# Sketched attention and a ReGLU feed-forward on one core: one interleaved program in place of two stages

## The chip, the core and the metric

The kernel runs on one core of a Trainium2 chip. A core has five engines that run side by side, each in its own order: PE (TensorE, matrix products into PSUM), DVE (VectorE), ACT (ScalarE), POOL (GpSimd) and SP (which here only issues transfers). The metric is the device time of one execution, in microseconds (us).

## What is computed

Queries, keys and values have 4 batches, 4 heads, 1088 tokens and 32 numbers a head. A sketch turns each head's 32 numbers into two vectors a and b of 8 numbers; their outer product is a feature vector of 64. Attention is linear in it, and its output is the input of a gated feed-forward layer (128 -> 1536 -> 128):

```python
def phi(x):
    a = np.einsum('rd,bhsd->bhsr', S1, x)
    b = np.einsum('rd,bhsd->bhsr', S2, x)
    return np.einsum('bhsi,bhsj->bhsij', a, b).reshape(*x.shape[:-1], r * r)
q_p, k_p = (phi(q), phi(k))
kv = np.einsum('bhsf,bhsd->bhfd', k_p, v)
z = np.sum(k_p, axis=2)
num = np.einsum('bhsf,bhfd->bhsd', q_p, kv)
den = np.einsum('bhsf,bhf->bhs', q_p, z)[..., None] + 1e-06
x = (num / den)            # then heads side by side: 4352 tokens x 128
out = (np.maximum(x @ w_gate, 0.0) * (x @ w_val)) @ w_out
```

## The kernel before

The program has two stages, and a scheduler orders the instructions of each engine.

**Attention** (L91 to L237) goes batch by batch. A batch's 1088 tokens are nine chunks, eight of 128 tokens and one of 64, with token s on partition s of its chunk; so the loads (L107 to L116) move runs of 32 numbers, 128 bytes each. For each key chunk PE transposes it as an fp32 matrix (L135), DVE copies the result out of PSUM (L137), PE applies the sketch (L140, an fp32 product, which stands as two matrix instructions in the trace), ACT copies that out (L142), POOL forms the outer products `kp` (L154), and PE adds up z (L144, `zbig`) and kv (L158) over the chunks. Between keys and queries ACT copies the sums out (L165 to L176) and PE folds z into the sketch matrix `s_bd_ext` (L172), so that the query product also yields what the denominator needs. Each query chunk then goes through transpose (L183), sketch (L188), outer product on POOL (L195), transpose of the features on PE (L202), copy on DVE (L208), product with kv (L211), the denominator (POOL L215, DVE L222, POOL L223, DVE L225), the division (DVE L228), another PE transpose (L236) and the copy into `xT` (ACT L237). `xT` is x with its 128 features on the partitions, for all 4352 tokens.

**Feed-forward** (L239 to L278) takes `xT` in chunks of 512 tokens (eight, and one of 256). For each of the 12 slices j of the 1536 hidden numbers: a gate product of 512 columns (L250), its ReLU on ACT (L252), a value product (L255), and on DVE the product of both into `ht` (L256). Twelve products with 512 columns each (L260) then give the output with its features on partitions; ACT copies it (L263), PE transposes it back in four pieces (L272), ACT scales it (L273), SP stores it (L275).

## Time and profile before

| | |
|---|---|
| runs | 224.64 and 225.14 us, median 224.89 |
| span of the profiled execution, first to last instruction | 223.3 us; so some 1.3 to 1.8 us of a run lie outside the span |
| busy in the span | PE 179.1, DVE 106.2, ACT 103.2, POOL 82.1 us |
| mean granted PE clock over the span | 0.973 |
| first PE instruction | at 14.2 us |
| first FFN product of the unbroken stretch | at 144.2 us |
| transfers | 61776 packets, 57152 of them under 512 bytes, 9.18 MB |

A busy share is the time in which an engine had an instruction in flight; matrix instructions overlap each other, so a busy PE may still have room. Rows of groups give, after the shapes and the count, busy us and the mean ns of one instruction, then the idle time ahead of them and who ended it. Rows of the timeline give start, length, engine and line.

### The profile page before, as it was taken

To read this page: it belongs to the slowest core of one execution; us is meant where nothing else is said; L and a number is where in the kernel's file an instruction comes from. 1 tells how busy PE (TensorE), PEld (TensorE's weight loads), DVE (VectorE), ACT (ScalarE), POOL (GpSimd) and SP (SyncE) were. 2 spreads that over 40 slices of the span, in tenths; PEclk is the share of its full clock that TensorE was granted. 3 is DMA by queue.
4 is the path that set the end of the run, shared out by engine and by line. 5 is a ranking of instruction groups with operands and counts; after the bars stand their busy time and mean duration, and the time that the engine had idled before them with its cause. 6 is when DMAs were issued, how large, how long until landed. Compare 5 with 4: busy or idle time off the path is not lost.

```text
span 223.3 us, 3087 instructions
## 1 busy us (share of the span) xinstructions
PE 179.1 (80%) x906; PEld 105.7 (47%) x906; DVE 106.2 (48%) x290; ACT 103.2 (46%) x307; POOL 82.1 (37%) x187
## 2 busy tenths in 40 slices
PE   0018999659949989689997795599999999999992
PEld 0005666437727667366674552234444444444460
DVE  0002003333114431224422154369998989989981
ACT  0021243112433213332234362158898988988981
POOL 8402578997378853158632385000000000000000
PEclk9999999999999999999999999559999999999998
DMA  7999989765494100000000000000110110110110
GB/s 95 156 125 135 156 107 84 72 23 44 72 52 72 28 0 0 3 0 1 0 1 3 0 0 1 0 0 3 47 48 0 47 51 0 47 42 6 50 47 23
DMA packets 61776, 9.18 MB, mean 41 GB/s; under 512 B 57152, under 2 KB 61504, under 8 KB 61760
## 3 DMA queue, kind: packets, MB, share of 16 engines
q1 hardware_dynamic: 39952, 6.69, 17.8%
q0 software_dynamic: 19568, 2.30, 17.0%
q10 hardware_dynamic: 2240, 0.01, 0.7%
q8 instruction: 7, 0.11, 0.2%
q14 instruction: 9, 0.07, 0.1%
HBM read 9.06 MB, written 2.23 MB: 51 GB/s over the span
## 4 chain that ended last, share of the span: by engine, by line
PE 60%; POOL 18%; DMA 7%; issue 5%; DVE 4%; ACT 4%; SPq 0%; ACTq 0%; POOLq 0%
PE v_ps L255 12%; PE ot_ps L260 10%; PE g_ps L250 10%; POOL qp L195 8%; PE ab_ps L140 7%; DMA k<-in_k_dram 4%; PE zbig_ps L144 4%; POOL den L223 3%; POOL bw L215 3%; PE tr_ps L183 3%; PE kv_ps L158 2%; DMA s_bd<-in_S_dram 2%; PE xtsz_ps L236 2%; PE ndq_ps L211 2%; PE ab_ps L188 2%
## 5 line engine op out<-in xcount | busy, mean ns | idle before, releaser
L256 DVE TENSOR_TENSOR ht<-g_sb,v_ps 128x512 f16<-128x512 f16 (+1 forms) x108 | 67.3, 656 | 8.1 <-PE v_ps L255 4.0
L252 ACT ACTIVATE g_sb<-g_ps 128x512 f16<-128x512 f32 (+1 forms) x108 | 59.1, 583 | 11.5 <-PE g_ps L250 7.9
L255 PE MATMUL v_ps<-xT,wv_sb 128*128 128x512 f16 (+1 forms) x108 | 40.7, 379 | 0.8 <-DVE ht L256 0.4
L250 PE MATMUL g_ps<-xT,wg_sb 128*128 128x512 f16 (+1 forms) x108 | 40.9, 382 | 0.0
L260 PE MATMUL ot_ps<-ht,wo_sb 128*128 128x512 f16 (+1 forms) x108 | 39.8, 374 | 0.2 <-DVE ht L256 0.2
L154 POOL TENSOR_TENSOR kp<-ab_sb 128x256 f16<-128x256 f32 (+1 forms) x36 | 22.2, 623 | 23.8 <-ACT ab_sb L142 20.6
L135 PE MATMUL tr_ps<-ident,k 128*128 128x128 f32 (+1 forms) x36 | 14.7, 435 | 17.8 <-DMA k<-in_k_dram 14.2
L188 PE MATMUL ab_ps<-s_bd_ext,tr_sb 128*128 128x96 f32 (+1 forms) x72 | 25.3, 455 | 4.5 <-ACT s_bd_ext L175 2.6
L195 POOL TENSOR_TENSOR qp<-ab_sb 128x256 f16<-128x256 f32 (+1 forms) x36 | 22.5, 625 | 13.1 <-ACT ab_sb L190 12.3
L142 ACT COPY ab_sb<-ab_ps 128x64 f32<-128x64 f32 (+1 forms) x36 | 7.6, 211 | 41.0 <-PE ab_ps L140 31.8
L140 PE MATMUL ab_ps<-s_bd,tr_sb 128*128 128x64 f32 (+1 forms) x72 | 23.5, 431 | 2.3 <-DMA s_bd<-in_S_dram 2.3
L188 PEld LDWEIGHTS ab_ps<-s_bd_ext,tr_sb 128*128 128x128 f32 (+1 forms) x72 | 17.1, 298 | 9.6 <-ACT ab_sb L190 5.4
L137 DVE COPY tr_sb<-tr_ps 128x128 f32<-128x128 f32 (+1 forms) x36 | 9.6, 275 | 25.4 <-PE tr_ps L135 21.9
L222 DVE TENSOR_REDUCE den<-bw 128x4 f32<-128x32 f32 (+1 forms) x36 | 6.6, 184 | 30.6 <-POOL bw L215 30.3
L190 ACT COPY ab_sb<-ab_ps 128x96 f32<-128x96 f32 (+1 forms) x36 | 8.6, 238 | 25.7 <-PE ab_ps L188 22.4
L140 PEld LDWEIGHTS ab_ps<-s_bd,tr_sb 128*128 128x128 f32 (+1 forms) x72 | 17.5, 305 | 4.7 <-issue 3.1
L208 DVE COPY qpt<-ndq_ps 128x256 f16<-128x256 f16 (+1 forms) x36 | 10.0, 277 | 17.8 <-PE ndq_ps L202 17.2
L135 PEld LDWEIGHTS tr_ps<-ident,k 128*128 128x128 f32 (+1 forms) x36 | 8.0, 229 | 20.9 <-issue 14.4
L250 PEld LDWEIGHTS <-wg_sb 128*128 128x128 f16 x108 | 11.1, 103 | 13.2 <-issue 4.7
L260 PEld LDWEIGHTS <-wo_sb 128*128 128x128 f16 x108 | 10.6, 98 | 14.1 <-issue 3.8
L255 PEld LDWEIGHTS <-wv_sb 128*128 128x128 f16 x108 | 10.7, 99 | 12.6 <-issue 2.9
L237 ACT COPY xT<-xtsz_ps 128x128 f16<-128x128 f16 (+1 forms) x36 | 9.4, 261 | 14.8 <-PE xtsz_ps L236 14.7
(44 smaller groups left out, 207.5 us busy)
## 6 DMA issues: line engine op xcount, KB each, us to landing
k<-in_k_dram SPq DMA_DIRECT2D x16, 128.0 KB, 3.5
q<-in_q_dram SPq DMA_DIRECT2D x16, 128.0 KB, 4.6
out_dram<-o_sb SPq DMA_DIRECT2D x8, 256.0 KB, 2.3
v<-in_v_dram POOLq DMA_DIRECT2D x16, 64.0 KB, 3.4
wg_sb<-in_moe_w_gate_dram POOLq DMA_DIRECT2D x1, 384.0 KB, 5.9
wv_sb<-in_moe_w_val_dram POOLq DMA_DIRECT2D x1, 384.0 KB, 7.5
wo_sb<-in_moe_w_out_dram POOLq DMA_DIRECT2D x1, 384.0 KB, 11.0
s_bd<-in_S_dram ACTq DMA_DIRECT2D x8, 1.0 KB, 5.6
```

The source lines that it names most:

```text
L135: nc.tensor.transpose(tr_ps[:, :c], k4[:c, ci].rearrange("s h d -> s (h d)"), ident[:c, :c])
L137: nc.vector.tensor_copy(out=tr_sb[:, :c], in_=tr_ps[:, :c])
L140: nc.tensor.matmul(ab_ps[:c, 0:2 * HR], tr_sb[:, :c], s_bd, start=True, stop=True)
L154: nc.gpsimd.tensor_tensor(out=kp[:c], in0=a_bc, in1=b_bc, op=ALU.mult)
L188: nc.tensor.matmul(ab_ps[:c], tr_sb[:, :c], s_bd_ext, start=True, stop=True)
L195: nc.gpsimd.tensor_tensor(out=qp[:c], in0=a_bc, in1=b_bc, op=ALU.mult)
L208: nc.vector.tensor_copy(out=qpt[:, :, :c], in_=qpt_ps[:, :, :c])
L250: nc.tensor.matmul(g_ps[:, :cs], wg_sb[:, j], xT[:, c0:c0 + cs], start=True, stop=True)
L252: nc.scalar.activation(out=g_sb[:, :cs], in_=g_ps[:, :cs], func=ACTF.Relu)
L255: nc.tensor.matmul(v_ps[:, :cs], wv_sb[:, j], xT[:, c0:c0 + cs], start=True, stop=True)
L256: nc.vector.tensor_tensor(out=ht[:, j, :cs], in0=g_sb[:, :cs], in1=v_ps[:, :cs], op=ALU.mult)
L260: nc.tensor.matmul(ot_ps[:, :cs], wo_sb[:, j], ht[:, j, :cs], start=(j == 0), stop=(j == NJ - 1))
```

## The change

The program is rewritten under a manual schedule: each engine runs its instructions in the order in which the source issues them.

- **Layout.** Of a batch, tokens 0 to 1023 are laid out eight to a partition (C = 8), so a load moves runs of 256 numbers, 1 KB each (`load_main`). The last 64 tokens of the four batches form one "rest" group of 256 tokens (`load_rest`). S1 is loaded 16 times (`s1r`).
- **Transposes.** fp32 matrix transposes on PE are replaced by 32x32 block transposes on DVE, before the sketch product (`t1`) and after it (`t2`), 512 columns at a time. The sketch product (`ab`) has the sketch as its weights and the transposed tokens as 512 fp32 columns.
- **Denominator.** It divides the vector a ahead of the outer product (`den`), so the product with kv yields x directly, with its features on the partitions, and `x` copies it into `xT`.
- **Feed-forward.** A token group is 512 tokens (two per batch), and a step `F` is two slices j: two gate and two value products of 512 columns, two ReLUs, one DVE product of 1024 columns. The output products take `ht` as weights and `wo` as 128 columns: eight for each step, which give the output with its tokens on partitions (`out`, two steps behind `gv`). The transposes back are gone. There are 48 such steps and three for the rest group.
- **Order.** The attention of the next group is cut into tasks, which `at` places at slots among these steps; whole slots come ahead of a step's `gv`, half slots between its `gv` and the `out` of two steps ago. All tasks take turns in one PSUM bank (`ps_m`).

Three places show what stands where now. First, the start on POOL. Before, the weights' transfers come ahead of all else; the names with numbers are buffers.

```order
L83 DMA wg_sb<-in_moe_w_gate_dram 128x1536
L85 DMA wv_sb<-in_moe_w_val_dram 128x1536
L87 DMA wo_sb<-in_moe_w_out_dram 128x12x128
L109 DMA v_150<-in_v_dram 128x8x32 x4
L113 DMA v_150<-in_v_dram 64x4x32
L129 COPY s_bd_ext<-s_bd 128x64 [waits DMAHW4_49,DMAHW5_49,DMAHW3_49,DMAHW6_49,DMAHW2_49,DMAHW7_49,DMAHW1_49,DVE_49]
```

Now a copy that waits for the loads of `s1r` stands ahead of them, and the first outer products (`kpr` of the rest group, `kp` of batch 0) behind them.

```order
L85 DMA v_sb_108<-in_v_dram 128x4x256
L120 COPY s1rep<-s1r 128x128 [waits DMAHW4_49,DMAHW6_49,DMAHW3_49,DMAHW7_49,DMAHW2_49,DMAHW0_49]
L121 DMA wg<-in_moe_w_gate_dram 128x1536
L122 DMA wv<-in_moe_w_val_dram 128x1536
L123 DMA wo<-in_moe_w_out_dram 128x12x128
L85 DMA v_sb_109<-in_v_dram 128x4x256
L85 DMA v_sb_110<-in_v_dram 128x4x256
L85 DMA v_sb_111<-in_v_dram 128x4x256
L176 TENSOR_TENSOR kpr<-abr 128x512 [waits DVE_49]
L176 TENSOR_TENSOR kp<-abk 128x512 [waits DVE_49]
```

So POOL's arithmetic moved behind six of its own transfers and one wait for ACT's.

Second, DVE in the feed-forward. Before, nothing stands among its products:

```order
L256 TENSOR_TENSOR ht<-g_sb,v_ps 128x512 [waits PE_49] x4
L256 TENSOR_TENSOR ht<-g_sb,v_ps 128x512 [waits PE_49,Activation_49] x92
L256 TENSOR_TENSOR ht<-g_sb,v_ps 128x256 [waits PE_49,Activation_49] x12
```

Now, for one query group (batch 1, first half; `abq` is `t2`, `dn` and `rd` belong to `den`, `pt` is `tre`):

```order
L263 TENSOR_TENSOR kv_bd_210<-m_ps,maskkv 128x128
L296 STREAM_TRANSPOSE qt<-q_sb_105 128x512 [waits DMAHW5_49]
L398 TENSOR_TENSOR ht<-g_sb,v_ps 128x1024 [waits DVE_49,PE_49,Activation_49]
L274 TENSOR_TENSOR wst_180<-m_ps,maskw 128x16x8 [waits PE_49,Pool_49]
L310 STREAM_TRANSPOSE abq<-m_ps 128x512
L320 TENSOR_REDUCE dn<-bw_184 128x16 [waits Pool_49]
L322 RECIPROCAL rd<-dn 128x16 [waits DVE_49]
L398 TENSOR_TENSOR ht<-g_sb,v_ps 128x1024 [waits PE_49,Activation_49] x2
L349 COPY pt<-m_ps 128x1024 [waits PE_49]
```

The attention's DVE work moved from ahead of the feed-forward to between its products, and each waits its turn behind a `ht`.

Third, PE. Before, only the output's own transposes stand among the feed-forward's products (`ot_2105` is one chunk's output):

```order
L250 LDWEIGHTS wg_sb
L250 MATMUL g_ps<-xT,wg_sb 128x512 [waits Activation_49]
L260 LDWEIGHTS wo_sb
L260 MATMUL ot_ps<-ht,wo_sb 128x512
L272 LDWEIGHTS ot_2105 [waits Activation_49]
L272 MATMUL ott_ps<-ident_96,ot_2105 128x128 [waits PE_49]
```

Now, at the same query group as above, the transposes of its features (`tr`, L339), which wait for POOL, stand behind a step's value products and ahead of the output products of two steps ago:

```order
L390 LDWEIGHTS wg
L390 MATMUL g_ps<-xT,wg 128x512 [waits Activation_49]
L395 LDWEIGHTS wv
L395 MATMUL v_ps<-xT,wv 128x512 [waits DVE_49]
L339 LDWEIGHTS qp [waits Pool_49]
L339 MATMUL m_ps<-ident,qp 128x128 [waits DVE_49]
L409 LDWEIGHTS ht
L409 MATMUL o_ps<-wo,ht 128x128
```

PE takes its instructions in this order, so all feed-forward products behind that L339 wait with it.

The core of the diff (the removed lines are the body of the kernel above; masks, identities and fills are left out):

```diff
+    ctx.enter_context(tc.manual_schedule())
...
+    ps_g = ctx.enter_context(tc.tile_pool(name="ps_g", bufs=2, space=bass.MemoryType.PSUM))
+    ps_v = ctx.enter_context(tc.tile_pool(name="ps_v", bufs=2, space=bass.MemoryType.PSUM))
+    ps_o = ctx.enter_context(tc.tile_pool(name="ps_o", bufs=1, space=bass.MemoryType.PSUM))
+    ps_m = ctx.enter_context(tc.tile_pool(name="ps_m", bufs=1, space=bass.MemoryType.PSUM))
...
+    def load_main(eng, dst, src, b):
+        eng.dma_start(out=dst, in_=src[b, :, 0:SM, :].rearrange("h (p c) d -> p h (c d)", c=C))
...
+    nc.scalar.dma_start(out=s16[0:R], in_=S1[:, None, :].to_broadcast([R, 4, D]))
+    nc.scalar.dma_start(out=s16[R:2 * R], in_=S2[:, None, :].to_broadcast([R, 4, D]))
+    load_rest(nc.sync, kr, k)
+    load_main(nc.sync, k_sb[0], k, 0)
+    load_main(nc.gpsimd, v_sb[0], v, 0)
+    load_rest(nc.scalar, vr32, v)
+    for x in range(128 // R):
+        nc.scalar.dma_start(out=s1r[x * R:(x + 1) * R], in_=S1)
+    load_main(nc.sync, q_sb[0], q, 0)
+    for b in range(1, B):
+        load_main(nc.sync, k_sb[b], k, b)
+        load_main(nc.sync, q_sb[b], q, b)
+    load_rest(nc.sync, qr, q)
...
+    nc.gpsimd.tensor_copy(out=s1rep, in_=s1r[:, None, :].to_broadcast([128, 4, D]))
+    nc.gpsimd.dma_start(out=wg, in_=moe_w_gate.rearrange("m (j f) -> m j f", j=NJ))
+    nc.gpsimd.dma_start(out=wv, in_=moe_w_val.rearrange("m (j f) -> m j f", j=NJ))
+    nc.gpsimd.dma_start(out=wo, in_=moe_w_out.rearrange("(j f) m -> f j m", f=128))
+    for b in range(1, B):
+        load_main(nc.gpsimd, v_sb[b], v, b)
...
+    def rest_k():
+        kt = a_t.tile([128, E * H * 32], FP32, name="ktr")
+        nc.vector.transpose(kt, kr.rearrange("p h (e d) -> p e h d", e=E))
+        ps = ps_g.tile([128, 512], FP32, name="g_ps")
+        nc.tensor.matmul(ps[:, 0:E * H * 32], sk[:, 0].rearrange("p a b f -> p (a b f)"), kt,
+                         start=True, stop=True)
+        nc.vector.transpose(abr.rearrange("p x f -> p (x f)"), ps[:, 0:E * H * 32])
+        outer(nc.gpsimd, kpr, abr, 0, R, E * H)
+    class K:
...
+        def t1(self, hf):
+            if hf == 0:
+                self.kt = a_t.tile([128, 2, GT], FP32, name="kt")
+            nc.vector.transpose(
+                self.kt[:, hf],
+                k_sb[self.b][:, :, hf * GC * D:(hf + 1) * GC * D].rearrange(
+                    "p h (c d) -> p c h d", d=D),
+            )
+        def ab(self, pool=ps_m, name="m_ps"):
+            self.ps = pool.tile([128, 512], FP32, name=name)
+            for hf in range(2):
+                nc.tensor.matmul(self.ps, sk[:, hf].rearrange("p a b f -> p (a b f)"),
+                                 self.kt[:, hf], start=(hf == 0), stop=(hf == 1))
+        def t2(self):
+            self.absb = a_ab.tile([128, GC * H, 32], FP32, name="abk")
+            nc.vector.transpose(self.absb.rearrange("p x f -> p (x f)"), self.ps)
+            self.kp = a_kp.tile([128, 2, GC * H, R * R], FP16, name="kp")
+        def phi(self, hf, eng, lo=0, hi=GC):
+            sl = slice(lo * H, hi * H)
+            outer(eng, self.kp[:, hf, sl], self.absb[:, sl], hf * 16, hf * 16 + R, (hi - lo) * H)
...
+        def kvz(self):
+            b = self.b
...
+                    nc.tensor.matmul(
+                        m[:, p * 64:p * 64 + 64],
+                        kpr[rows, e * H + 2 * p:e * H + 2 * p + 2].rearrange("s h f -> s (h f)"),
+                        vr[rows, 2 * p:2 * p + 2, e * D:(e + 1) * D],
+                        start=first, stop=False, skip_group_check=True)
...
+                        ab = self.absb[:, c * H:(c + 1) * H]
+                        nc.tensor.matmul(
+                            m[:, 128:192].rearrange("f (a h j) -> f a h j", a=2, h=H),
+                            ab.rearrange("s h f -> s (h f)"),
+                            ab.rearrange("s h (a f) -> s a h f", a=2)[:, :, :, R:2 * R],
+                            start=False, stop=c == GC - 1, skip_group_check=True)
...
+        def evac(self):
+            self.zd = a_sm.tile([128, 2 * H * R], FP32, name="zd")
+            nc.vector.tensor_tensor(
+                out=self.zd, in0=self.m[:, 128:192],
+                in1=maskz.rearrange("p a h j -> p (a h j)"), op=ALU.mult)
...
+        def w(self):
+            b = self.b
+            for hf in range(2):
+                nc.tensor.matmul(self.m[:, 192:224], s1rep.rearrange("p a d -> p (a d)"),
+                                 self.zd[:, hf * H * R:(hf + 1) * H * R],
+                                 start=hf == 0, stop=hf == 1)
...
+            nc.vector.tensor_tensor(
+                out=wst[b][:, :, :, 2 * R:3 * R],
...
+    class Q:
...
+            src = q_sb[self.b][:, :, g * GC * D:(g + 1) * GC * D] if self.b < B else qr
+            nc.vector.transpose(self.qt, src.rearrange("p h (c d) -> p c h d", d=D))
+        def ab(self, pool=ps_m, name="m_ps"):
+            n = self.n
+            self.ps = pool.tile([128, 512], FP32, name=name)
+            for h in range(H):
+                nc.tensor.matmul(
+                    self.ps[:, h * n * 32:(h + 1) * n * 32],
+                    wst[self.b][:, h].rearrange("p a f -> p (a f)"), self.qt[:, :, h, :],
+                    start=True, stop=True)
+        def t2(self):
+            n = self.n
+            self.absb = a_ab.tile([128, n * H, 32], FP32, name="abq")
+            nc.vector.transpose(
+                self.absb.rearrange("p (c h) f -> p c h f", h=H),
+                self.ps[:, 0:n * 128].rearrange("p (h c t) -> p c h t", h=H, c=n))
+        def den(self, eng):
+            n = self.n
+            x = n * H
+            eng.tensor_tensor(out=self.bw[:, 0:x, 0:R], in0=self.absb[:, :, R:2 * R],
+                              in1=self.absb[:, :, 2 * R:3 * R], op=ALU.mult)
+            dn = a_sm.tile([128, x], FP32, name="dn")
+            nc.vector.tensor_reduce(out=dn, in_=self.bw[:, 0:x], axis=AX.X, op=ALU.add)
+            rd = a_sm.tile([128, x], FP32, name="rd")
+            nc.vector.reciprocal(out=rd, in_=dn)
+            self.a = a_sm.tile([128, x, R], FP32, name="an")
+            eng.tensor_tensor(out=self.a, in0=self.absb[:, :, 0:R],
+                              in1=rd[:, :, None].to_broadcast([128, x, R]), op=ALU.mult)
+            self.qp = a_kp.tile([128, x, R * R], FP16, name="qp")
+        def phi(self, eng, lo=0, hi=None):
...
+            outer(eng, self.qp[:, sl], self.absb[:, sl], 0, R, (hi - lo) * H, a=self.a[:, sl])
+        def tr(self, pool=ps_m, name="m_ps"):
...
+            m = pool.tile([128, 512], FP32, name=name)
+            self.ps = m.bitcast(FP16)[:, 0:2 * n * 128].rearrange("f (p c t) -> f p c t", p=2, c=n)
+            for c in range(n):
+                for p in range(2):
+                    nc.tensor.transpose(
+                        self.ps[:, p, c],
+                        self.qp[:, c * H + 2 * p:c * H + 2 * p + 2].rearrange("s h f -> s (h f)"),
+                        ident)
...
+        def num(self, pool=ps_m, name="m_ps"):
...
+                if self.b < B:
+                    nc.tensor.matmul(o, kv_bd[self.b][:, p], self.pt[:, p].rearrange(
+                        "f c t -> f (c t)"), start=True, stop=True)
...
+        def x(self):
+            nc.scalar.copy(out=xT[:, self.col:self.col + self.n * 128],
+                           in_=self.ps[:, 0:self.n * 128])
...
+    class F:
...
+        def gv(self):
...
+            g_sb = f_g.tile([128, 2, 512], FP16, name="g_sb")
+            for bank in range(2):
+                g_ps = ps_g.tile([128, 512], FP32, name="g_ps")
+                for y, j in enumerate(self.js[bank]):
+                    nc.tensor.matmul(g_ps[:, y * W:(y + 1) * W], wg[:, j], x, start=True, stop=True)
+                nc.scalar.activation(out=g_sb[:, bank], in_=g_ps, func=ACTF.Relu)
+            v_ps = ps_v.tile([128, 2, 512], FP32, name="v_ps")
+            for bank in range(2):
+                for y, j in enumerate(self.js[bank]):
+                    nc.tensor.matmul(v_ps[:, bank, y * W:(y + 1) * W], wv[:, j], x,
+                                     start=True, stop=True)
+            self.ht = f_h.tile([128, 2, 512], FP16, name="ht")
+            nc.vector.tensor_tensor(out=self.ht, in0=g_sb, in1=v_ps, op=ALU.mult)
...
+        def out(self):
...
+            for bank in range(2):
+                for y, j in enumerate(self.js[bank]):
+                    for s in range(ns):
+                        nc.tensor.matmul(
+                            o[:, s], self.ht[:, bank, y * W + s * 128:y * W + (s + 1) * 128],
+                            wo[:, j], start=(j == 0 and s == 0), stop=(j == NJ - 1),
+                            skip_group_check=True)
...
+            nc.scalar.mul(out=o_sb[:, 0:ns], in_=o[:, 0:ns], mul=1.0 / (XSCALE * XSCALE))
...
+    k0 = kk[0]
+    k0.t1(0)
+    k0.t1(1)
...
+    nc.gpsimd.memset(wst[B], 0.0)
+    fill_static(nc.gpsimd, wst[B])
+    k0.w()
+    q0.ab(ps_g, "g_ps")
+    q0.t2()
+    q0.den(nc.vector)
+    q0.phi(nc.vector, 0, 2)
+    q0.phi(nc.gpsimd, 2, 4)
+    q0.tr(ps_g, "g_ps")
+    q0.tre(nc.vector)
+    q0.num()
+    q0.x()
...
+    for b in range(1, B):
+        s = start[b, 0]
+        kb = kk[b]
+        at(s - 11, kb.t1, 0)
+        at(s - 11, kb.t1, 1)
+        at(s - 10, kb.ab)
+        at(s - 9.5, kb.t2)
+        at(s - 9.5, kb.phi, 0, nc.gpsimd)
+        at(s - 9.5, kb.phi, 1, nc.gpsimd)
+        at(s - 6.5, kb.kvz)
+        at(s - 6, kb.evac)
+        at(s - 5.5, kb.w)
+    for key, s in start.items():
+        qk = qq[key]
+        if key == (0, 0):
+            continue
+        s = s if key[1] == 0 else s - 2.5
+        at(s - 6, qk.t1)
+        at(s - 5, qk.ab)
+        at(s - 4.5, qk.t2)
+        at(s - 4.5, qk.den, nc.gpsimd)
+        at(s - 4.5, qk.phi, nc.gpsimd)
+        at(s - 2.5, qk.tr)
+        at(s - 2.5, qk.tre, nc.vector)
+        at(s - 2, qk.num)
+        at(s - 2, qk.x)
...
+    LAG = 2
+    for s in range(len(steps) + LAG):
+        for fn, args in tasks.get(s, []):
+            fn(*args)
+        if s < len(steps):
+            steps[s].gv()
+        for fn, args in tasks.get(s + 0.5, []):
+            fn(*args)
+        if s >= LAG:
+            steps[s - LAG].out()
```

More of the change, by code (lines that the diff above doesn't have):

```diff
@@ L14 @@
 ACTF = mybir.ActivationFunctionType
+AX = mybir.AxisListType
 XSCALE = 1.0 / 16.0
+DSCALE = 1.0 / 16.0
+KVSCALE = XSCALE * DSCALE
+EPS = 1e-6
 @with_exitstack
@@ new lines @@
+    for key, s in start.items():
[12 more added lines that the diff above has]
+        at(s - 2, qk.x)
+    at(0, fill_wst)
+    for s in sorted(t for t in tasks if t < 0):
+        for fn, args in tasks[s]:
+            fn(*args)
```

410 lines of the change are left out of this document (216 added, 194 removed).

## The prediction

> **What bounds the kernel now.** First the busy time of each engine by stage (columns: stretch, its length, then busy us of PE, PE's weight loads, DVE, ACT and POOL, the granted clock, the share of the transfer engines, GB/s).
>
> ```profile
> 0.00:14.00 14.00, 0.00 (x0) 0.00 (x0) 0.24 (x2) 0.00 (x0) 7.52 (x16) 1.00 1.17 130
> 30.00:126.00 96.00, 79.80 (x430) 56.71 (x428) 28.62 (x135) 29.83 (x148) 60.03 (x136) 1.00 0.35 29
> 136.00:140.00 4.00, 1.38 (x15) 0.67 (x12) 1.98 (x9) 0.83 (x4) 1.41 (x5) 0.96 0.00 0
> 140.00:144.00 4.00, 2.02 (x13) 1.01 (x13) 1.38 (x5) 0.62 (x3) 0.00 (x0) 0.50 0.00 0
> 144.00:150.00 6.00, 5.47 (x13) 1.86 (x13) 3.35 (x5) 2.94 (x6) 0.00 (x0) 0.50 0.00 0
> 150.00:212.00 62.00, 61.94 (x294) 27.21 (x293) 57.77 (x89) 54.44 (x102) 0.00 (x0) 1.00 0.11 31
> ```
>
> Three stages with three bounds: 14 us of loading; 130 us of attention (14 to 144), in which DVE and ACT are under a third busy; 79 us of feed-forward, in which PE never pauses. Then the timeline of PE:
>
> ```profile
> 85.23 0.42 PE L202 MATMUL ndq_ps<-ident,qp 128*128 128x128 f16 x2
> 134.16 0.41 PE L188 MATMUL ab_ps<-s_bd_ext,tr_sb 128*128 128x96 f32 x2
> 134.41 0.38 PE L250 MATMUL g_ps<-xT,wg_sb 128*128 128x512 f16 x1
> 139.24 0.28 PE L202 MATMUL ndq_ps<-ident,qp 128*128 128x128 f16 x2
> 140.65 0.42 PE L202 MATMUL ndq_ps<-ident,qp 128*128 128x128 f16 x2
> 189.43 0.39 PE L272 MATMUL ott_ps<-ident,ot 128*128 128x128 f16 x4
> 193.76 0.38 PE L260 MATMUL ot_ps<-ht,wo_sb 128*128 128x512 f16 x1
> 193.98 0.38 PE L255 MATMUL v_ps<-xT,wv_sb 128*128 128x512 f16 x1
> 194.19 0.38 PE L250 MATMUL g_ps<-xT,wg_sb 128*128 128x512 f16 x1
> ```
>
> The same pair of L202 takes 0.28 us at 139.24 (granted clock about 1) and 0.42 at 140.65 (granted 0.50). At 85.23 it takes 0.42 too, though the clock column says 1.00 there: I read the attention stage as run at half clock, whatever the column says. So PE's prices in it are halved where the clock is full. In the feed-forward, products of 512 columns start 0.215 us apart (193.76, 193.98, 194.19).
>
> **The change, part by part: prices.** The rows, one group each (busy us, mean ns):
>
> ```profile
> L256 DVE TENSOR_TENSOR ht<-g_sb,v_ps 128x512 f16<-128x512 f16 x96 | 62.5, 686 | 7.3 <-PE v_ps L255 3.7 <-ACT g_sb L252 2.4 <-PE g_ps L250 0.3
> L256 DVE TENSOR_TENSOR ht<-g_sb,v_ps 128x256 f16<-128x256 f16 x12 | 4.7, 419 | 0.8 <-PE v_ps L255 0.2
> L252 ACT ACTIVATE g_sb<-g_ps 128x512 f16<-128x512 f32 x96 | 55.0, 608 | 10.8 <-PE g_ps L250 7.2 <-DVE ht L256 2.1
> L195 POOL TENSOR_TENSOR qp<-ab_sb 128x256 f16<-128x256 f32 x32 | 20.0, 626 | 13.0 <-ACT ab_sb L190 12.3
> L215 POOL TENSOR_TENSOR bw<-ab_sb 128x32 f32<-128x32 f32 x32 | 8.0, 250 | 1.4
> L222 DVE TENSOR_REDUCE den<-bw 128x4 f32<-128x32 f32 x32 | 5.9, 185 | 30.0 <-POOL bw L215 30.0
> L225 DVE RECIPROCAL rden<-den 128x4 f32<-128x4 f32 x32 | 5.6, 176 | 15.2 <-POOL den L223 14.9
> L137 DVE COPY tr_sb<-tr_ps 128x128 f32<-128x128 f32 x32 | 8.7, 281 | 22.7 <-PE tr_ps L135 20.2 <-PE ab_ps L140 2.4
> L137 DVE COPY tr_sb<-tr_ps 128x64 f32<-128x64 f32 x4 | 0.9, 222 | 2.7 <-PE tr_ps L135 1.7 <-PE ab_ps L140 0.9
> L208 DVE COPY qpt<-ndq_ps 128x256 f16<-128x256 f16 x32 | 9.1, 284 | 15.5 <-PE ndq_ps L202 14.8
> L263 ACT CAST ot<-ot_ps 128x512 f16<-128x512 f32 x8 | 4.7, 582 | 0.0
> ```
>
> - `ht` of 1024 columns: 686-419 ns for 256 more gives 1.04 ns a column, so 0.686+0.534 = 1.22 us. Two ReLUs: 1.22 us.
> - POOL's products: 626-250 ns for 224 more columns, 1.67 ns each: 1.91 us for 1024, 1.05 for 512, 0.41 for 128.
> - A 32x32 transpose of 512 fp32 columns has no row. From below the copies (281-222 ns for 64 more, 0.92 each): 0.63 us; from above twice that. I take 0.63, since it reads and writes as the copy does. `pt`, 1024 columns: at L208's 1.1 ns a column 1.1 us from above; half of that from below, if the fixed part is most of the 284; I take 0.65. Reduction 0.30, reciprocal 0.18, `x` 0.58.
> - fp32 products on PE: the pair L188 with 96 columns holds PE from 134.16 to 134.41, 0.25 us. With 128 columns I take 0.3. With 512 columns the bounds are 0.43 (two passes at 0.215) and 1.7 (eight); I take four, 0.9.
> - fp16 products of 128 columns with new weights: four of L272 in 0.39 us, one of them 0.22, so 0.057 apart. Eight output products: 0.45 us.
>
> A step is then 4 x 0.215 + 0.45 = 1.31 us of PE, 1.22 of DVE, 1.22 of ACT. Over 512 tokens that is 7.9 us where 36 products take 7.7 now: the token-major output gives nothing back by itself. The gain is that the 130 us stage goes in between.
>
> [...]
>
> **The period.** A batch is 12 steps: 15.7 us of PE. Its keys add 2 x 0.9 (`ab`), 20 fp16 products at 0.045, six fp32 pairs (`kvz`) and two (`w`) at 0.25: 4.7. Each half's queries add 4 x 0.3, 8 x 0.057 and 2 x 0.215: 2.1. Sum 24.6 us; DVE's is 22, so PE would bound it, if it never waited. But `m_ps` is one bank, and PE takes its queue in order. I walk the queues; hops between engines, by these rows, cost 0.02 to 0.05:
>
> ```profile
> 139.90 0.30 PE ndq_ps L211 x2
> 140.22 0.30 DVE x_sb L228
> 140.57 0.29 PE xtsz_ps L236
> ```
>
> - `tr` of the first half: after `ab`, DVE must first do that step's `ht` (ReLUs end 1.6 after `gv` starts, `ht` at 2.8), then `t2` 3.45, `bw` 3.86, reduction and reciprocal 4.34, `an` 4.75, outer product 6.66, six hops 7.0. PE arrives after three `gv` and two `out`, 3.5. It waits **3.5 us**; everything behind it on PE waits too, and ACT and DVE run dry.
> - `tr` of the second half: the same chain ends 5.35 after `ab`, PE arrives at 3.07: **2.3**.
> - `kvz`: two outer products end 7.4 after `ab`, PE needs the second at 6.2: **1.2**. First `ab` of the queries: `wst` stands behind a `ht` and ends at 3.6, PE arrives at 2.3: **1.3**. `num` waits for `pt` 0.45 twice, the keys' `ab` for `x` 0.45: **1.35**.
>
> Waits 9.7, period **34.3 us**, three of them: 103. Ahead of them two steps with a wait for the second half of batch 0: 6.8. Behind them 13 steps, 17.0, the rest group's 1.4, its waits 2.2: 20.6.
>
> **Start and end.**
>
> ```profile
> 0.95 0.40 ACTq L72 DMA_DIRECT2D s_bd<-in_S_dram  x1
> 4.57 0.71 ACTq L72 DMA_DIRECT2D s_bd<-in_S_dram  x1
> 1.60 0.78 POOL L83 DMA_DIRECT2D wg_sb<-in_moe_w_gate_dram  x1
> 2.37 0.56 POOL L85 DMA_DIRECT2D wv_sb<-in_moe_w_val_dram  x1
> 2.90 1.07 POOL L87 DMA_DIRECT2D wo_sb<-in_moe_w_out_dram  x1
> 3.92 3.54 POOL L109 DMA_DIRECT2D v<-in_v_dram  x4
> 17.13 0.24 POOL L129 COPY s_bd_ext<-s_bd 128x64 f32<-128x64 f32 x1 [9.04 <-DMA s_bd<-in_S_dram]
> k<-in_k_dram SPq DMA_DIRECT2D x4, 32.0 KB, 2.5
> 220.44 0.37 SPq L275 DMA_DIRECT2D out_dram<-o_sb  x1
> ```
>
> ACT issues one load each 0.60 us (0.95 to 4.57 is six). Now there are 22; the last is issued by 14.2 and lands 2.5 later, 16.7. POOL then copies (0.24), issues three weight loads (2.4) and three of v (0.9 each, 2.7): 22.0. Only then come its three products of 512, 25.1. The larger runs of k and q, which should land well before, are hidden behind this. Then `kvz`'s rest, `evac`, `w`, `wst` 3.5; `ab` at half clock 2.4; `t2` and `den` 1.6; outer product 1.05; `tr`, `pt`, `num`, `x` 2.6; the next `ab` 2.4, hops 0.6: first `gv` at **39 us**. At the end: ReLUs and `ht` 2.05, `out` 0.65, scaling 0.4, four stores issued at 0.4 each, and from the last issue to the span's end 2.1 (220.44+0.37 to 223.3 is 2.5 with landing): **6.8**.
>
> **Clock.** After four thin microseconds (136 to 140, PE 1.38 busy) the clock stood at 0.50 for ten. Waits of 3.5 and 2.3 in each period may do it again; I take 2 us a period, 6, with 0 and the rival below as bounds.
>
> Sum: 39 + 6.8 + 103 + 20.6 + 6.8 + 6 = 182 against a span of 223.3. The two runs are 1.3 to 1.8 us above that span, so **184 us** against a median of 224.9.
>
> **Rivals.**
> 1. *The waits are mostly hidden.* If POOL's wide products cost less than the line through 32 and 256 columns says, `tr` finds its data: period 26, start 35: 182 - 25 - 4 = 153, so 155. For: only widths up to 256 were seen. Against: the chain has four more members.
> 2. *Half clock throughout, slower than before.* If the waits in each period keep PE's clock at 0.50, as the thin stretch at 136 did, PE's 24.6 become 49 and hide nearly all waits: periods of 50, ahead 10, behind 36, start and end 46: 242, so 244. It turns slower than 224.9 once some 65% of the interleaved part runs so. For: the whole attention stage ran so. Against: dense products raised it again at 150, and with PE the bound it has no waits to thin it out.
>    [...]
> 3. *Transposes at twice the price.* Each `t2` on a chain and the `t1` ahead add 0.63, about 3.5 a period and 3 at the start, with `pt` at its upper bound 3 more a period: 182+22 = 204, so 206. For: no row of the operation. Against: nothing but that.
>
> That the change does not do what it says is excluded: the order lists show attention tasks between the steps.
>
> **How the numbers follow.** Forecast 0.62 (164 to 200), rival 1 0.20, rival 2 0.08, rival 3 0.10. The range takes in rivals 1 and 3 and the prices' bounds (fp32 at 1.7 adds 1.6 to 2 a period and the start, the second `ab` another; early loads take 6 off): 152 to 214. Faster by over 2%, about what a measurement can tell from no change (under 220.4): 0.62 + 0.20 + 0.09 = 0.91. Slower by over 2%: 0.06 of rival 2; within: 0.03.
>
> **What would show it.** The first `gv` near 39 us, behind POOL's products; 34 us between the `kvz` of two batches; L339 waiting some 3.5 and 2.3 us for POOL; transposes of 0.63 us; output products 0.057 apart. Wrong if L339 hardly waits (rival 1), if the clock reads 0.50 for most of the loop (rival 2), if DVE is over 80% busy (rival 3).

## The result and the profile after

The changed kernel takes 186.62 us (median of two runs, 185.89 and 187.36) against 224.89 before: a ratio of 0.830, 95% interval 0.822 to 0.838. The forecast was 184. Single runs of one kernel spread by up to 5%; the times below are medians of all its runs, and the ratios leave disturbed runs out.

The head of the page after, with the granted clock in 40 slices:

```profile
span 185.7 us, 2481 instructions
PE 129.6 (70%) x951; PEld 82.6 (44%) x951; DVE 96.7 (52%) x148; ACT 66.1 (36%) x122; POOL 50.0 (27%) x65
PEclk9998555558597897887988978999999699999798
```

Before, the three stages kept PE busy for 179.1 us of 223.3; now it is 129.6 of 185.7. No engine is near its limit: PE stands at 70%, DVE at 52%. By stretches (length, busy us of PE, PEld, DVE, ACT and POOL, then the granted clock): the start, the two steps ahead of the first keys' `ab`, three periods from one keys' `ab` to the next, and the rest:

```profile
0.00:38.98 38.98, 16.27 (x70) 11.24 (x70) 11.42 (x40) 2.27 (x3) 13.20 (x26) 0.72 0.83 176
38.98:46.82 7.84, 4.38 (x19) 1.35 (x18) 5.45 (x8) 2.76 (x5) 5.78 (x9) 0.72 0.01 2
46.82:85.95 39.13, 31.68 (x221) 19.70 (x221) 21.44 (x29) 14.61 (x27) 9.94 (x10) 0.81 0.02 8
85.95:121.35 35.40, 28.32 (x222) 18.21 (x221) 20.64 (x29) 15.22 (x29) 9.68 (x9) 0.90 0.04 16
121.35:154.90 33.55, 26.17 (x216) 16.73 (x217) 19.55 (x26) 14.52 (x28) 9.69 (x9) 0.95 0.05 17
154.90:185.70 30.80, 22.74 (x212) 15.34 (x209) 18.16 (x19) 16.70 (x33) 1.69 (x3) 0.93 0.09 31
```

The first `gv` starts at 38.98. The three periods hold the same work and take 39.1, 35.4 and 33.6 us; PE's busy time and the clock move with them, so the same products were slower in the first. The clock's records read 1.00 or 0.50, so a mean of 0.81 over 39.13 us is 2 x 0.19 x 39.13 = 15 us at half clock; the five stretches behind the start make 34 us that way. The last 1.1 of them lie at the end, where PE has no more work, and the first 2.2 belong to a stretch that began in the start, so that 31 us of half clock began in the loop.

What PE waited for (us in all, times, the longest):

```profile
PE m_ps L339 <- POOL qp L176: 19.6, 8, 3.2
PE m_ps L251 <- POOL kp L176: 3.4, 3, 1.2
PE m_ps L302 <- DVE wst L274: 3.0, 3, 1.2
PE m_ps L357 <- DVE pt L349: 0.8, 1, 0.8
```

And one such wait, in the timeline of the first half of the second batch:

```profile
64.13 1.16 PE L302 MATMUL m_ps<-qt,wst 128*128 128x128 f32 x8 [1.03 <-DVE wst L274]
66.66 1.22 DVE L398 TENSOR_TENSOR ht<-g_sb,v_ps 128x1024 f16<-128x1024 f16 x1 [2.58 <-ACT g_sb L391]
67.80 0.71 DVE L310 STREAM_TRANSPOSE abq<-m_ps 128x512 f32<-128x512 f32 x1
68.65 0.46 POOL L317 TENSOR_TENSOR bw<-abq 128x128 f32<-128x128 f32 x1 [4.24 <-DVE abq L310]
69.14 0.30 DVE L320 TENSOR_REDUCE dn<-bw 128x16 f32<-128x144 f32 x1 [0.64 <-POOL bw L317]
69.48 0.25 DVE L322 RECIPROCAL rd<-dn 128x16 f32<-128x16 f32 x1
69.81 0.41 POOL L324 TENSOR_TENSOR an<-abq,rd 128x128 f32<-128x128 f32 x1 [0.70 <-DVE rd L322]
70.30 1.95 POOL L176 TENSOR_TENSOR qp<-an,abq 128x1024 f16<-128x1024 f32 x1
72.30 1.03 PE L339 MATMUL m_ps<-ident,qp 128*128 128x128 f16 x8 [3.23 <-POOL qp L176]
```

`ab` (L302) ends at 65.29. Its transpose starts only at 67.80, behind a `ht` that itself stood idle 2.58 us for its ReLUs. Then six members follow one another, and PE, which arrived at 69.07, goes on at 72.30. The row says that it waits for POOL's `qp`; the part that could be spared is at the other end of the chain, in front of DVE's transpose.

### The profile page after: what moved, and what is told of

Read it like the earlier page. It is cut to its first block, busy times and chain, and to the rows that moved or that the text cites. A ratio compares the mean times of both kernels' runs of the same rounds, so it can differ in the third digit from the quotient of the medians.

```text
span 185.7 us, 2481 instructions
## 1 busy us (share of the span) xinstructions
PE 129.6 (70%) x951; PEld 82.6 (44%) x951; DVE 96.7 (52%) x148; ACT 66.1 (36%) x122; POOL 50.0 (27%) x65
## 5 line engine op out<-in xcount | busy, mean ns | idle before, releaser
L398 DVE TENSOR_TENSOR ht<-g_sb,v_ps 128x1024 f16<-128x1024 f16 x51 | 60.5, 1207 | 37.9 <-ACT g_sb L391 31.5
L391 ACT ACTIVATE g_sb<-g_ps 128x512 f16<-128x512 f32 x102 | 55.2, 595 | 58.1 <-PE g_ps L390 58.1
L390 PE MATMUL g_ps<-xT,wg 128*128 128x512 f16 (+1 forms) x108 | 35.4, 406 | 0.6
L409 PE MATMUL o_ps<-wo,ht 128*128 128x128 f16 x408 | 34.0, 231 | 1.0 <-DVE ht L398 1.0
L395 PE MATMUL v_ps<-xT,wv 128*128 128x512 f16 (+1 forms) x108 | 33.7, 401 | 0.0
L409 PEld LDWEIGHTS <-ht 128*128 128x128 f16 x408 | 28.9, 105 | 10.1 <-issue 2.1
L176 POOL TENSOR_TENSOR kp<-abk 128x1024 f16<-128x1024 f32 (+1 forms) x8 | 13.7, 1734 | 24.2 <-DVE abk L215 24.2
L339 PE MATMUL m_ps<-ident,qp 128*128 128x128 f16 x60 | 5.9, 254 | 19.6 <-POOL qp L176 19.6
L395 PEld LDWEIGHTS <-wv 128*128 128x128 f16 x108 | 11.3, 105 | 16.2 <-issue 7.3
L176 POOL TENSOR_TENSOR qp<-an,abq 128x1024 f16<-128x1024 f32 (+1 forms) x9 | 16.3, 1810 | 4.6 <-DVE an L324 4.0
L339 PEld LDWEIGHTS <-qp 128*128 128x128 f16 x68 | 4.9, 114 | 26.6 <-POOL qp L176 23.5
L210 PE MATMUL m_ps<-kt,sk 128*128 128x512 f32 x16 | 11.5, 858 | 1.9 <-DVE kt L201 1.1
L302 PE MATMUL m_ps<-qt,wst 128*128 128x128 f32 (+1 forms) x64 | 9.8, 301 | 4.0 <-DVE wst L274 3.0
L302 PEld LDWEIGHTS m_ps<-qt,wst 128*128 128x128 f32 x64 | 9.0, 212 | 5.9 <-DVE wst L274 3.5
L260 DVE TENSOR_TENSOR zd<-m_ps,maskz 128x64 f32<-128x64 f32 x4 | 0.9, 224 | 17.6 <-PE m_ps L251 17.6
```

The source lines that it names most:

```text
L176: eng.tensor_tensor(out=dst.rearrange("s x (i j) -> s x i j", i=R), in0=a_src[:, :, :, None].to_broadcast([128, n, R, R]), in1=ab[:, :, No ...
L210: nc.tensor.matmul(self.ps, sk[:, hf].rearrange("p a b f -> p (a b f)"), self.kt[:, hf], start=(hf == 0), stop=(hf == 1))
L302: nc.tensor.matmul(self.ps[:, h * n * 32:(h + 1) * n * 32], wst[self.b][:, h].rearrange("p a f -> p (a f)"), self.qt[:, :, h, :], start=Tr ...
L339: nc.tensor.transpose(self.ps[:, p, c], self.qp[:, c * H + 2 * p:c * H + 2 * p + 2].rearrange("s h f -> s (h f)"), ident)
L390: nc.tensor.matmul(g_ps[:, y * W:(y + 1) * W], wg[:, j], x, start=True, stop=True)
L391: nc.scalar.activation(out=g_sb[:, bank], in_=g_ps, func=ACTF.Relu)
```

## Experiments

The names e1 to e11 are those that the expectations use.

**All attention first (e4).** What is the interleaving worth, and what the rest of the change?

```
-    for s in sorted(t for t in tasks if t < 0):
-        for fn, args in tasks[s]:
+    for s in sorted(tasks):
+        for fn, args in tasks.pop(s):
```

> Edit: all attention tasks are issued ahead of the first feed-forward step, in their old order among themselves; nothing else changes, so the wide products, the 32x32 transposes, the layout of 8 tokens and the token-major output stay. Theory (the gain comes from putting the two stages into each other): three rounds of attention of 27-30 us behind the 39 of the start, one half ahead and the rest group behind (13), then 51 steps of 1.31 and the end: 205-222. Rival (the gain comes from the cheaper attention, and interleaving adds little): 186-195.

Measured: 229.6 us in one run, no faster than before the change (226.0 in the same session). Two of its three attention periods and the feed-forward alone, by stretches, and its main wait:

```profile
46.74:79.08 32.34, 16.83 (x77) 11.73 (x77) 7.75 (x16) 1.17 (x2) 9.93 (x10) 1.00 0.00 1
...
111.34:143.00 31.66, 16.84 (x76) 11.74 (x76) 6.94 (x15) 0.61 (x2) 9.66 (x9) 0.50 0.00 0
150.00:220.00 70.00, 69.21 (x600) 42.68 (x597) 59.42 (x50) 58.11 (x109) 0.00 (x0) 0.96 0.07 28
```

```profile
PE m_ps L339 <- POOL qp L176: 34.5, 8, 4.5
```

The theory holds and more: the time is above its range, because the periods took 32 us and not 27 to 30. A batch of attention alone takes as long as the 130 us of four batches before (32.5 each), although PE is busy for 16.8 us of it only: the row shows PE waiting for POOL's chain, and this run does not tell by how much one bank for all of it adds to that. The feed-forward alone is as long as before too (first `gv` at 150.0, span 227.9). So all of the gain is the interleaving: the same program without it is 43 us longer.

The rows also settle how to read the clock. The same 76 or 77 products are busy for 16.83 us where the column says 1.00 and for 16.84 where it says 0.50. The first record of a clock event stands at 83.4 us in this trace; ahead of it the column shows 1.00 and means nothing. In the trace of the kernel before, the first record stands at 132.9, so its 1.00 over the attention stage means nothing either, and the prediction's reading of half clock there, from the pair of L202 (0.42 us there, 0.28 under a record of 1.00), stands.

**The chain half a step earlier (e2).**

```
-        at(s - 4.5, qk.t2)
-        at(s - 4.5, qk.den, nc.gpsimd)
-        at(s - 4.5, qk.phi, nc.gpsimd)
+        at(s - 5, qk.t2)
+        at(s - 5, qk.den, nc.gpsimd)
+        at(s - 5, qk.phi, nc.gpsimd)
```

> Edit: t2, den and phi of the queries are issued half a step earlier, ahead of the next step's ht on DVE, instead of behind it. Theory (PE waits in front of L339 because t2 stands behind a ht that itself waits for its ReLUs: in the first half of the second batch, `ab` ends at 65.3 and t2 starts at 67.8): the chain ends 2.5 us earlier in each group, PE's waits in front of L339 fall from 19.6 us to under 5, some of the half-clock stretches go with them, and the time falls to 168-175. Rival A (the bank m_ps makes the chain serial, so the wait turns up at the next use of the bank, in front of L302, L210 or L357): 182-187. Rival B (DVE is late next: ht is pushed behind the reduction, PE waits in front of L409 or L390): 182-190.

Measured: 176.9 us (four runs, the lowest 175.2), just above the theory's range.

```profile
PE m_ps L339 <- POOL qp L176: 11.9, 7, 2.8
```

```profile
68.36 0.62 PE L339 MATMUL m_ps<-ident,qp 128*128 128x128 f16 x8 [0.77 <-POOL qp L176]
77.39 0.62 PE L339 MATMUL m_ps<-ident,qp 128*128 128x128 f16 x8 [2.27 <-POOL qp L176]
```

The waits in front of L339 fell by 7.7 us and not by 15. Those of the first halves went from 3.2 to 0.77. Those of the second halves, 1.7 to 2.0 in the three periods of the changed kernel, became 2.27, and there the theory overlooked a line of its own table: their `ab` is issued behind the `gv` of its step, so `t2` stands behind that step's `ht` whatever its slot. Neither rival: no other row of PE's waits grew by more than 1.0.

**POOL's product twice (e3).** The same chain, lengthened:

```
         at(s - 4.5, qk.phi, nc.gpsimd)
+        at(s - 4.5, qk.phi, nc.gpsimd)
```

> Edit: POOL computes each outer product of the queries (L176, 1.95 us for 1024 columns) twice, for the eight groups behind the first. Theory (POOL's chain sets when PE goes on): seven products of 1.95 and one of about 1.1 stand on the path, 14 to 15 us: 200-203, with the waits in front of L339 at 33-35 us. Rival (the bubbles are covered: what PE loses there it makes up, since ACT and DVE catch up meanwhile): under 192.

Measured: 210.0 us in one run, and

```profile
PE m_ps L339 <- POOL qp L176: 33.8, 8, 5.6
```

The waits grew by 14.2 us, as expected. The time grew by 22 to 23, beyond the theory's range: half clock in the loop went from 31 to 58 us by the trace's clock records, which the theory had not counted.

**The waits filled with work (e5).** Is it the waiting that brings the half clock, and what does that cost by itself?

```
+FILL = 9
...
             m = pool.tile([128, 512], FP32, name=name)
+            for x in range(FILL if pool is ps_m else 0):
+                nc.tensor.matmul(m, ident, wg[:, 0:4].rearrange("m j f -> m (j f)"), start=True, stop=True)
```

> Edit: ahead of each group's transposes L339, where PE waits for POOL, it runs nine products of 512 columns whose result nobody reads (1.9 us at full clock, 3.9 at half). They add work to PE and take no wait away. Theory (PE's idle stretches bring the half clock, and half clock costs: from the runs so far 0.3 us for each of the 31 us of it in the loop): half clock in the loop falls from 31 us to under 10, the time from 186.6 to 178-182, though PE does 16 us more. Rival (the half-clock stretches have another cause, or cost nothing): half clock stays near 30 us, time 186-192.

Measured: 179.2 us (176.8 to 182.1), ratio to before 0.784 (0.779 to 0.788). Seventy-two useless products of 512 columns make the kernel some 7 us faster by the medians, 10 by the ratios. What PE still waits for there, and the clock by slices, to be held against the rows after the change:

```profile
PE m_ps L342 <- POOL qp L177: 4.8, 6, 1.3
PE m_ps L252 <- POOL kp L177: 3.5, 3, 1.2
PEclk9999999999997899999969999999799999999996
```

By the trace's clock records, half clock in the loop fell from 31 to 10 us, in three stretches that begin 0.1 to 1.1 us behind the waits of `kvz` (L252, 1.15 us each). So PE's waits in front of L339 brought most of the half clock. An estimate of its price follows: the waits fell by 14.8 us and the useless products add 15.5 (72 at 0.215), so that 20.5 us less of half clock brought 8 to 11, 0.4 to 0.5 us for each. In the run with the doubled product 27 us more of it cost 22.6 (span) - 14.2 = 8.4, 0.3 us for each.

**Where the start hangs (e1, e6, e9).** First, POOL's copy of `s1rep` behind the first keys' products:

```
-    nc.gpsimd.tensor_copy(out=s1rep, in_=s1r[:, None, :].to_broadcast([128, 4, D]))
     nc.gpsimd.dma_start(out=wg, in_=moe_w_gate.rearrange("m (j f) -> m j f", j=NJ))
...
     k0.phi(1, nc.gpsimd, 2, 4)
+    nc.gpsimd.tensor_copy(out=s1rep, in_=s1r[:, None, :].to_broadcast([128, 4, D]))
     k0.kvz()
```

> Edit: POOL's copy of s1rep, which only `w` reads, is issued behind the four products of the first keys instead of ahead of the weight loads. Theory (the start hangs on ACT's sixteen s1r loads: the copy starts at 16.4 us, and with it everything queued behind it on POOL): POOL's first products start some 6 to 8 us earlier (22.3 to about 15), the first gv comes at 31 to 33 us instead of 39.0, and the time falls from 186.6 to 179-181. Rival A (the loads bound the start: 9 MB share the transfer engines, and weights that are issued earlier only push the others back): first gv at 37 or later, time 185-187. Rival B (the wait is only moved, `w` or `kvz` waits for the same transfers): as A, with the wait in front of L271.

Measured: 182.4 us, ratio 0.806 (0.803 to 0.809), first `gv` at 35.66. The timeline shows why only half of it came:

```profile
8.14 9.12 ACTq L101 DMA_DIRECT2D s1r<-in_S_dram  x11
...
13.99 2.62 POOL L175 TENSOR_TENSOR kp<-abk 128x512 f16<-128x512 f32 x2 [3.86 <-DVE abk L214]
14.14 3.03 DVE L175 TENSOR_TENSOR kp<-abk 128x512 f16<-128x512 f32 x2
18.59 0.41 ACT L455 CAST vr<-vr 128x256 f16<-128x256 f32 x1
19.05 0.26 PE L228 MATMUL m_ps<-vr,kpr 32*128 32x64 f16 x2 [5.89 <-ACT vr L455]
```

POOL's products start 8 us earlier and are done at 17.2, but `kvz` then waits for ACT's cast of `vr`, which stands behind the same sixteen loads on ACT. ACT is through with issuing them at 17.3 here and was at 13.4 in the changed kernel, where POOL's transfers start later; there the cast had ended at 15.1, and nothing waited for it. So the loads were taken off ACT as well; POOL's copy stays behind the first keys' products:

```
-        nc.scalar.dma_start(out=s1r[x * R:(x + 1) * R], in_=S1)
...
     load_rest(nc.sync, qr, q)
+    for x in range(128 // R):
+        nc.sync.dma_start(out=s1r[x * R:(x + 1) * R], in_=S1)
```

> Edit: as in e1_s1rep_late, and the sixteen s1r loads are issued by SP behind the loads of q and k instead of by ACT, whose cast of vr waited behind them there until 18.6. Theory (after e1 the start hangs on that cast): the first `kvz` starts at about 17.3 (22.4 after the change, 19.05 in e1), the first gv at 33.5-34.5, time 180-182. Rival (the s1r loads are now too late, `w` waits for s1rep, or v_sb for its transfer): first gv at 36 or later, time 183-186.

Measured: 194.7 us (191.1 to 201.0), slower than the changed kernel, and first `gv` at 48.35. The first half of the theory came true (`kvz` at 13.81), the queue chosen for the loads undid it:

```profile
6.39 6.45 SPq L85 DMA_DIRECT2D q_sb<-in_q_dram  x1
17.84 5.33 SPq L89 DMA_DIRECT2D qr<-in_q_dram  x4
23.20 11.49 SPq L106 DMA_DIRECT2D s1r<-in_S_dram  x16
36.17 0.29 POOL L467 COPY s1rep<-s1r 128x128 f32<-128x128 f32 x1 [19.80 <-DMA s1r<-in_S_dram]
```

With some 4 MB of k, q, v and weights issued ahead of it, SP stood 6.45 us in a single issue (0.4 for the first ones), and came to `s1r` at 23.2. Last, one load in place of sixteen, on ACT, again with the copy behind the first keys' products:

```
-    for x in range(128 // R):
-        nc.scalar.dma_start(out=s1r[x * R:(x + 1) * R], in_=S1)
+    nc.scalar.dma_start(out=s1r, in_=S1[None, :, :].to_broadcast([128 // R, R, D]))
```

> Edit: the sixteen s1r loads become one load that reads S1 sixteen times, still issued by ACT behind the loads of vr; POOL's copy of s1rep stands behind the first keys' products as in e1. The rest is the changed kernel. Theory (the first 39 us hang on s1r: in e6 it was taken off ACT, and `kvz` began at 13.8 and `evac` at 18.2, but on SP the loads came only at 23.2, since SP's issues there take 2 to 6 us each): `evac` at 18.2, and since the first gv came 12.3 behind `evac` (26.67 to 38.98), first gv at 30 to 31.5, time 175-181. Rival (wg, wv or the queries' loads are late next): first gv at 34 or later, time 182-187.

Measured: 175.6 us (173.4 to 177.7), ratio 0.777 (0.775 to 0.780), and the first `gv` 8.1 us earlier:

```profile
30.84 1.06 PE L388 MATMUL g_ps<-xT,wg 128*128 128x512 f16 x2
```

The start did hang on the sixteen loads, through POOL and through ACT. The medians differ by 11 us; where the other 3 come from is not shown. Less half clock it is not: behind the first `gv` the clock records of the profiled runs have 34 us of it here and 33 in the changed kernel.

**The table of slots written anew (e7).** One bank, `m_ps`, serves all attention tasks in program order. In the changed kernel `ab` and the transposes that need its POOL chain are neighbours in that order. Here another task stands between them, the distance from `ab` to the transposes grows from 2.5 steps to 4, and the second batch's `ab` moves into the start:

```
+    k1.ab()
+    k1.t2()
...
-        at(s - 10, kb.ab)
-        at(s - 9.5, kb.t2)
...
-        at(s - 6.5, kb.kvz)
...
-        at(s - 5.5, kb.w)
+        if b > 1:
...
+            at(s - 16, kb.ab)
+            at(s - 16, kb.t2)
...
+        at(s - 11, kb.kvz)
...
+        at(s - 10, kb.w)
...
-        s = s if key[1] == 0 else s - 2.5
...
-        at(s - 5, qk.ab)
-        at(s - 4.5, qk.t2)
...
-        at(s - 2.5, qk.tr)
...
-        at(s - 2, qk.num)
...
+        at(s - 6, qk.ab)
+        at(s - 6, qk.t2)
...
+        at(s - 2, qk.tr)
...
+        at(s - 1, qk.num)
```

> Edit: only the table of slots is written anew: no POOL chain stands between two uses of m_ps that follow each other. The keys' `ab` is issued 16 steps ahead of their batch and `kvz` 11 (10 and 6.5 now), the queries' `ab` 6, their transposes 2, `num` 1 step ahead, in both halves alike; t2 right behind `ab`; the second batch's keys go into the idle time of the start. Theory (the bank m_ps is used in one order, and its chain of `ab`, POOL's products, transposes, `num` adds up to more than PE's 24.6 us a period; put in an order in which each result has a step or more of time, the waits go and PE bounds the period): periods of 26-28 us, waits in front of L339 and L251 under 4 us in sum, hardly any half clock behind the first gv, time 149-160. Rival A (the bank bounds the period in any order): periods of 31 or more, 168-176. Rival B (DVE, 22 us of work in a period of 26, is late next): waits in front of L409 or L390, 160-168.

Measured: 144.5 us (143.9 to 145.8), ratio 0.640 (0.636 to 0.644): below the theory's range. Two periods, and all that PE still waits for behind the first `gv`:

```profile
53.50:79.84 26.34, 24.59 (x220) 16.60 (x221) 21.53 (x29) 15.20 (x28) 9.68 (x10) 1.00 0.06 22
79.84:106.00 26.16, 25.55 (x226) 17.05 (x227) 21.35 (x28) 15.68 (x30) 9.51 (x10) 1.00 0.06 21
```

```profile
PE m_ps L210 <- DVE kt L201: 3.7, 3, 1.3
PE m_ps L357 <- DVE pt L349: 1.9, 8, 0.8
PE o_ps L409 <- DVE ht L398: 1.0, 1, 1.0
```

(1.1 of the first row and 0.8 of the second lie in the start.) L339 waits no longer in the loop, the clock is 1.00, and the same work runs in 26.3 us a period (the second stretch holds two gate and two value products more). Of 43 us against the changed kernel, 24 are waits (all of PE's above 0.25 us behind the first `gv`: 27.9 then, 3.6 now), 1.6 an earlier first `gv`, and some 2 the second batch's `ab`, which found PE idle in the start. What is left, 15, is no more than the half clock behind the first `gv` can have cost at half its 33 us; all of that is gone but some 1.5 us (the last 36.5 us read 0.98). One bank is enough; how the tasks followed each other in it was not. Order and distance were changed together here, and the slot of `t2` with them, which the run with the chain half a step earlier shows to matter in the old order too. DVE, at 21.5 of 26.3, is not late either.

**Table and start together (e8, e10).** Once with the loads on SP, once with the one load; in both POOL fills the static part of `wst` ahead of the first keys' products.

> Edit: e6 and e7 together, with the static part of wst filled by POOL ahead of the first keys' products. Theory (start and loop are independent): e7's time less what e6 gains over the changed kernel, 144-155. Rival (with an earlier first step the loads of the later batches or the fills on POOL come too late): within 1 us of e7.

> Edit: e9 and the table of e7 together, wst filled by POOL ahead of the first keys' products as in e8. Theory (start and loop add): in e8 the first gv came 10.5 behind `w` (35.4 to 45.9); `w` comes at 18.5 here, so first gv at 29, 8.4 earlier than in e7, time 134-138. Rival (v or k of the second batch, or wo, arrives too late for a loop that starts at 29): waits in front of L409, L251 or L229 behind the first gv, time 139-145.

Measured: 154.0 us (152.8 to 158.1) with the loads on SP, where `w` waits 17.6 us for `s1rep` as above. With the one load 139.3 us (136.4 to 141.4), ratio 0.606 (0.603 to 0.609), 136.9 by that ratio: the fastest kernel here. The median lies in the rival's range, but the waits that the rival asks for are not there: behind the first `gv` PE waits no more than with the table alone.

```profile
0.00:29.58 29.58, 15.85 (x74) 9.79 (x74) 14.99 (x43) 2.27 (x3) 20.65 (x34) 0.88 1.09 230
45.70:72.04 26.34, 24.59 (x220) 16.58 (x221) 21.53 (x29) 15.20 (x28) 9.67 (x10) 1.00 0.06 22
```

The period is the same 26.34, the start 7.8 shorter: start and loop add.

**The output feature-major again (e11)**, in the new table: two products of 512 columns a step, and at the end of a half a copy, four transposes, the scaling.

```
+                    nc.tensor.matmul(o[:, 0:W], wo[:, j], self.ht[:, bank, y * W:(y + 1) * W],
+                                     start=(j == 0), stop=(j == NJ - 1))
...
+            nc.scalar.copy(out=ot[:, 0:W], in_=o[:, 0:W])
...
+                nc.tensor.transpose(tt[:, s], ot[:, s * 128:(s + 1) * 128], ident)
```

> Edit: e7 with the output of the feed-forward feature-major, as before the change: two products of 512 columns a step instead of eight of 128, and at the end of each half a copy by ACT, four transposes on PE through a bank of g_ps, and the scaling from there. Theory (in an order of tasks in which PE never waits, the end of a half costs a wait: the copy stands on ACT behind two ReLUs, and PE takes nothing else in the meantime): 1.5 to 2 us for each of eight halves and the rest group, 155-162 against e7's 144.5, with waits in front of the transposes. Rival (the count of the prediction, by which the form of the output gives nothing back: 0.43 for 0.45 us a step, less 1 us in all, and 0.4 a half for the transposes): 143-148.

Measured: 154.0 us (152.8 to 154.7), 9.4 above the same table with the token-major output, and below the theory's range. PE waits, and pays for 34 transposes:

```profile
PE g_ps L418 <- ACT ot L414: 5.9, 9, 0.7
PE g_ps L390 <- ACT o_sb L419: 1.9, 4, 0.5
```

The mechanism is the theory's, with 0.7 us a half where it had 1.5 to 2, and a second wait that it had not: `gv` for the bank that the scaling still reads. 1.0 us of the 9.4 lies in the start. The rival, which is the prediction's own count, is wrong: in this loop, in which PE otherwise hardly waits, the form of the output is worth some 8 us. Whether the transposes, put elsewhere, would cost less was not tried.

## Why the prediction held, point by point

- **The start, 39 us: right to 0.02.** The mechanism was half told. It named POOL's queue behind `s1r`, and that was what set the time; the cast of `vr` on ACT, next in line behind the same loads, was missed. Whoever had moved only the copy, by the prediction, would have gained 3.3 us at the first `gv` and not 8.
- **The period's work, 24.6 us of PE: right.** The new table shows 26.3 with 1.6 of waiting (1.3 in front of L210, 0.3 of L357), so 24.7. Two prices in it were the author's estimates, with no row before: 0.9 for an fp32 product of 512 columns and 0.045 for an fp16 product of `kvz`. In the changed kernel, at a record of 1.00, two of the first took 1.98 us together (at 121.35) where 1.8 was counted, and all of `kvz` without its wait took 2.49 (128.23 to 131.87, less 1.15) where 2.4 was.
- **The waits, 9.7 a period: 7.1 on the mean** (7.3, 6.9, 7.3). One by one: first halves 3.5, measured 3.23; second halves 2.3, measured 2.77, 2.03, 1.70 and 1.70; `kvz` 1.2, measured 1.04 to 1.16; `wst` 1.3, measured 0.76 to 1.17. The step that failed is the last: 0.9 for `num` on `pt` and 0.45 for the keys' `ab` on `x`. The eight output products between `tr` and `num` cover `pt` (its row has a single wait of 0.8, in the start), and the keys' `ab` waited for `x` once, 0.68, ahead of the first period.
- **The clock, 6 us: too small.** The periods less 24.7 of work and their waits leave 7.1, 3.8 and 1.6, so 12.5. It was sized by a guess of 2 a period between 0 and the rival; by the clock's records the three periods had 14.8, 6.8 and 3.4 us at half clock.
- **Ahead 6.8, behind 20.6, end 6.8:** 7.8, about 23 (the rest group waits 1.65 for POOL at 169 and runs 3.4 us at half clock behind it), 7.7.

So the forecast had 8 us of waits too many, 6 of clock too few and 4 at the ends too few: the sum of 182 came within 4 us of the span partly because its errors cancel, and that part is luck.

- **The prices.** Transposes, and POOL's products:

```profile
L296 DVE STREAM_TRANSPOSE qt<-q_sb 128x512 f32<-128x512 f32 x8 | 5.6, 702 | 0.0
L176 POOL TENSOR_TENSOR qp<-an,abq 128x1024 f16<-128x1024 f32 x7 | 13.7, 1951 | 0.5
```

A transpose took 0.70 where the copies gave 0.63, POOL's product 1.95 where the line through 32 and 256 columns gave 1.91. Rival 3 (1.26 a transpose) is out by the first row, rival 1 (cheap wide products) by the second. Eight output products start within 0.39 us (0.61 less the 0.22 of the last): 0.056 apart, as forecast. Four fp32 products of 128 columns took 1.16 us, 0.29 each, where 0.3 was taken.
- **Rival 2, half clock throughout,** came true in 31 us of 139. The clock rose to 1.00 again each time: of the eight stretches of half clock that began in the loop ahead of the end, seven lasted 3.4 us and one 6.8. Three of them begin within 0.4 us of the ends of the three waits of 3.23 (at 71.90, 109.45 and 143.58, the waits ending at 72.30, 109.17 and 143.34); but with those waits filled, stretches of half clock still began at waits of 1.15. In the row from 136 to 140 before the change PE's longest wait is 0.98 us, and the clock's records read 0.50 from 139.7 on: half clock stood there behind thin work (PE 1.38 us busy of 4) without a long wait.
- **"The gain is that the 130 us stage goes in between": right**, and sharper than it was put: without the interleaving the change gains nothing (one run, 1.6% longer than the kernel before).
- **"The token-major output gives nothing back by itself"** holds for this kernel's two stages, where the feed-forward alone is as long as before; it was an argument on busy time, and in the new table, where PE hardly waits, it is wrong by some 8 us.

Not separated: the layout of 8 tokens per partition and the 32x32 transposes, each by itself. The run without interleaving shows them together with the rest only.

## What to carry to other kernels

When two stages are put into each other on one in-order queue, write down the order in which they use each shared buffer, and let no long chain on another engine stand between two neighbours in it: here a new table of slots, by itself, was worth 42 us of 187, more than the whole change. Waits can cost more than their length: here 14.2 us of added waits, with 27 us more of half clock, cost 22.6, so their sum was a lower bound. And look for everything that is queued behind a small load, on each engine that issues or awaits it: one load in place of sixteen, with the copy that awaits it moved back, gave 11 us.
